# An early activation and a new order for the first stage of a kernel of chunked attention and two feed-forward layers

## The chip, the cores and the metric

The kernel runs on one core of a Trainium2 chip. The metric is the device time of one execution in microseconds (us). Three executions of the kernel before took 1139.6, 1143.71 and 1144.55 us; the median is 1143.71. A core has TensorE (PE: products; its loads of weights are PEld), VectorE (DVE), ScalarE (ACT), GpSimd (POOL) and SyncE (SP, whose queue issues nearly all loads). Each works through its own list of instructions in order and waits for others by semaphores.

## The reference

Three parts follow one another. First, attention in chunks of 32 queries with 16 keys to the left, 8 to the right and 8 memory keys, for 4 batches, 8 heads, 768 positions and 64 channels per head:

```python
for c in range(nc):
    k_full = np.concatenate([mem_k, k_ctx], axis=2)      # 8 + up to 56 keys
    scores = scale * np.matmul(q_c, k_full.transpose(0, 1, 3, 2))
    a = np.exp(scores - np.max(scores, axis=-1, keepdims=True))
    a = a / (np.sum(a, axis=-1, keepdims=True) + 1e-09)
    out[:, :, c_start:c_end] = np.matmul(a, v_full)
```

Its result, seen as x with 3072 rows of 512, goes through two feed-forward layers with 2048 hidden channels:

```python
h = x @ w_in                                  # 3072x512 @ 512x2048
g = s * np.maximum(h, 0.0) ** 2 + b           # first layer
x = g @ w_out                                 # 2048x512
h = x @ moe2_w_in
g = np.maximum(h, 0.0) + alpha * np.minimum(h, 0.0)   # second layer
y = g @ moe2_w_out
```

The weights come as 64-bit floats.

## The kernel before, in words

**Tiles and blocks.** The 3072 rows are 24 tiles of 128 rows, and 6 blocks of four tiles (512 rows). Attention is made tile by tile; the feed-forward layers work on a block at a time. The hidden channels are cut into 16 pieces of 128, called f below. One unit is one block with one piece: a first product (`g1`, line 633, ph), the activation (lines 644 to 677: g, then a high half gh and a low half gl), and a second product (`g2`, lines 692 and 694) that adds to the four banks po. Each product is made of three, high times low, low times high and high times high, so that a unit has 12 matmuls of 512 columns in `g1` and 12 in `g2`. The second product of a unit is placed two units after its first (`LAG`).

**The weights.** A piece has a half for the first product ("w3i" in the lists) and one for the second ("w3o"); pieces 0 and 1 are loaded and converted half by half, the others whole (1.05 MB). `convert` (line 286) turns the 64-bit words into a high and a low 32-bit part in seven steps: magnitude (ScalarE, line 296), clamp, shift, low, sign (VectorE, lines 299, 304, 309, 314), high (ScalarE, line 321) and rest (VectorE, line 327). Two conversions at most can be under way, as their temporary tile has two buffers.

**The attention of a tile.** Loads q (queries and keys, 0.64 MB, lines 376 and 377) and v (0.52 MB, line 384); scores on TensorE (line 401, 128 instructions of TensorE); maxima (line 419), exponentials, sums, reciprocals and normalising (line 475) on VectorE and ScalarE; a turn on TensorE (line 466), copied by ScalarE (line 471); values on TensorE (line 488, 128 instructions); the high half of x by ScalarE (line 520), the low half by VectorE (line 524). A tile in `BY_HEAD` makes its exponentials head by head on ScalarE (line 452, eight activations which also give the sums), another in one activation of 512 columns (line 433) with a subtraction (line 429) and a sum (line 437) on VectorE. There are four sets of buffers for q and v; tile i uses set i mod 4 among the first eight tiles, so v7 needs tile 3's values to be done. Sets 2 and 3 lie in the places of the weights of pieces 13, 14 and 15.

**The first stage.** It makes tiles 0 to 3 (block 0) one by one, then tiles 4 to 7 (block 1) in joint steps of TensorE, each with the scores of one tile and the values of the tile before. The units of block 0 with pieces 0, 1 and 2 (`HALVES`) are cut into a left half of columns, which needs tiles 0 and 1 only, and a right half, which needs tiles 2 and 3. Then come the other pieces below `SEG` for block 0, then all pieces below `SEG` for block 1 (nothing new to convert there), then the pieces from `SEG` on for block 0 and for block 1. Between, the partial sums of both blocks are spilled and later added. From block 2 on all 16 pieces are there, and attention is made two tiles at a time beside the products.

**What sets the order.** All steps are put into a `Plan`, each with its engine, its estimated cost, a rank, and what it waits for. `Plan.order()` (line 147) runs through the plan with these costs and always takes the step that can start first on each engine, ties and readiness by rank (a lower rank goes first). The resulting list is the program's order on each engine. SP's queue is different: it is in order of rank alone, and for the first stage that is the order of `FIRST_LOADS` (line 46). `TILE_RANKS`, `CONV_RANKS` and `STEPS` shift the ranks of the attention tiles, of the conversions and of the steps within a tile. `RATE` is the planner's rate of loads in bytes per us. `Pace` (line 83) is its picture of TensorE: a clock that is slow until a window was busy, and instructions that are fetched in blocks of 256, the first boundary after 184; at each boundary TensorE waits until the block has come, `FETCH` us after it was asked for, by the first figure when no load is under way and by the second when one is. None of these figures is an instruction of the program; they act through the order alone.

Of the kernel before, what the change touches and what calls it, by code (L numbers as in the profile page):

```python
# [9 lines left out]
F32 = mybir.dt.float32  # L10
F32R = mybir.dt.float32r
U32 = mybir.dt.uint32
ACTF = mybir.ActivationFunctionType
# [3 lines left out]
P = 128  # L17
# [14 lines left out]
NEG = -1.0e30  # L32
SCALE = 1.0 / float(D) ** 0.5

SEG = 7
LAG = 2
HALVES = 3
PIECES = 2
# [4 lines left out]
SET_SLOTS = {2: 15, 3: 14}  # L43
QA_SLOT = 13

FIRST_LOADS = """q0 q1 w1i v0 q3 w0o q2 v2 w0i v1 w1o q4 v3 w2 w3 w4 v4 w6 q5 v7 q6 v5 q7 w5 w9 v6 w7 w8""".split()

TILE_RANKS = (-280, -85, -170, -175, -15, -240, -5, -260, -85)

BY_HEAD = (1, 2, 4, 5, 6)  # L50

CONV_RANKS = {1: 195, 2: 35, 3: 30, 4: 25, 5: 20, 6: 15, 9: -40, 10: -95, 11: -25, 12: -10, 13: 40, 14: -70}

STEPS = (28, 18, 18, 47, 43, 38)


KHEAD = LEFT + RIGHT
# [25 lines left out]
class Pace:  # L83


    WINDOW, PHASE = 3.41, 2.7
    BLOCK, FIRST = 256, 184

    def __init__(self):
        self.window, self.active, self.warm = 0, 0.0, False  # L90
# [11 lines left out]
    def run(self, t, step, fetch):  # L102

        done, total = 0, max(step.count, 1)
        while done < total:
            at = self.count + done
            block, into = divmod(at - self.FIRST, self.BLOCK)
            if block >= 0 and into == 0:
                t = max(t, self.due[block])
                self.due[block + 1] = t + fetch(t)  # L110
            n = min(total - done, self.BLOCK - into)
            work = step.cost * n / total
            while work > 1e-9:
                self._to(t + 1e-6)
                speed = 1.0 if self.warm else 0.65 if step.dense else 0.53
                left = self.PHASE + (self.window + 1) * self.WINDOW - t
                took = min(left, work / speed)
                self.active += took * (0.5 if step.dense else 1.0)
                work -= took * speed
                t += took  # L120
            done += n
        self.count += total
        return t


class Plan:
# [1 line left out]

    PAST = {"PE": 0.22, "DVE": 0.15, "ACT": 0.2, "POOL": 0.15, "SP": 2.2, "PQ": 2.2}
    NEXT = {"DVE": 0.12, "ACT": 0.12}  # L130
    RATE = 396e3
    LANES = 8
    FETCH = 2.7, 5.3

    def __init__(self, rings):
        self.steps = []
# [10 lines left out]
    def order(self):  # L147
        for s in self.steps:
            s.n_wait = len(s.after)
            for a in s.after:  # L150
                a.outs.append(s)
        engines = {s.engine for s in self.steps}
        open_ = {e: [] for e in engines}
        for s in self.steps:
            if not s.n_wait:
                open_[s.engine].append(s)
        at = {e: 0.0 for e in engines}
        last = {}
        held = {}
        wire = 0.7  # L160
        landed = [0.0] * self.LANES
        pace = Pace()
        due = sorted((s for s in self.steps if s.engine == "SP"), key=lambda s: (-s.rank, -s.seq))
        done = []
        while len(done) < len(self.steps):
            best = None
            for e in engines:
                pick = None
                queue = [due[-1]] if e == "SP" and due else open_[e]
                for s in queue:  # L170
                    if s.n_wait:
                        continue
                    r = s.ready
                    if s.takes:
                        free = self.free[s.takes[0]]
                        if not free:
                            continue
                        r = max(r, min(free.values()))
                    r = max(r, at[e] + (self.NEXT[e] if e in self.NEXT and last.get(e) in s.after else 0.0))
                    if e == "SP" and s.bytes:  # L180
                        r = max(r, landed[-self.LANES])
                    key = (max(r, at[e] + 0.02), s.rank, s.seq)
                    if pick is None or key < pick[0]:
                        pick = (key, r, s)
                if pick and (best is None or pick[1] < best[1]):
                    best = pick
            assert best, [(e, s.rank, s.takes, s.seq) for e in engines for s in open_[e]]
            _, t, s = best
            e = s.engine
            open_[e].remove(s)  # L190
            if e == "SP":
                due.pop()
            slot = None
            if s.takes:
                ring, holder = s.takes
                free = self.free[ring]
                slot = min(free, key=lambda n: (free[n], n))
                del free[slot]
                held[holder] = (ring, slot)
            s.start = t  # L200
            last[e] = s
            at[e] = pace.run(t, s, lambda t: self.FETCH[wire > t + 1.0]) if e == "PE" else t + s.cost
            end = at[e]
            if s.bytes:
                n = max(1, s.bytes >> 18)
                for k in range(n):
                    wire = max(wire, t + s.cost * (k + 1) / n) + s.bytes / n / self.RATE
                    landed.append(wire + self.PAST[e])
                end = wire
            s.end = end + self.PAST[e]  # L210
            for holder in s.frees:
                ring, n = held.pop(holder)
                self.free[ring][n] = s.end
            for o in s.outs:
                o.n_wait -= 1
                o.ready = max(o.ready, at[e] if o.engine == e in ("PE", "DVE", "ACT") else s.end)
                if not o.n_wait:
                    open_[o.engine].append(o)
            done.append((s, slot))
        return done  # L220
# [3 lines left out]
def tile_chunk_attention_two_ffn(ctx: ExitStack, tc: tile.TileContext, qt, kw, vw, win, wout, cst, out):  # L224
    nc = tc.nc
    const = ctx.enter_context(tc.tile_pool(name="const", bufs=1))
# [13 lines left out]
    plan = Plan({"ph": 2, "g": 2, "gg": 3, "ao": 2})  # L240
# [7 lines left out]
    units = [(0, 0, f, left) for f in range(HALVES)] + [(0, 0, f, right) for f in range(HALVES)]  # L248
    units += [(0, 0, f, full) for f in range(HALVES, SEG)]
    units += [(0, 1, f, full) for f in range(SEG)]  # L250
    units += [(0, j, f, full) for j in range(2) for f in range(SEG, KF)]
    units += [(layer, j, f, full) for layer in range(2) for j in range(2 * (1 - layer), NB) for f in range(KF)]
# [18 lines left out]
    def groups(f):  # L271
        return ((0,), (1,)) if f < SPLIT else ((0, 1),)
# [10 lines left out]
    def first_load(name):  # L283
        return -1000.0 + FIRST_LOADS.index(name)

    def convert(layer, f, mats, rank, after):
# [42 lines left out]
        name = f"w{f}" + ("io"[mats[0]] if n == 1 else "")  # L329
        load = plan.add("SP", 0.45 * n, first_load(name) if layer == 0 and name in FIRST_LOADS else rank - 60 + 14 * mats[0], lambda: load_part(layer, f, mats), after, nbytes=n * (1 << 19))  # L330
        load_done[key] = load
# [198 lines left out]
    def softmax(i, r, sc):  # L530
        a = att[i]
        mx = plan.add("DVE", (0.8 if i % TB in (0, TB - 1) else 0.61) + (0.08 if i in ALONE else 0), r + STEPS[0], lambda: maxima(i), [sc])
        if i in BY_HEAD:
            nm = plan.add("DVE", 0.1, r + STEPS[0], lambda: negate(i), [mx])
            ex = None
            for hp in range(HP):
                ex = plan.add("ACT", 0.58, r + STEPS[1], lambda hp=hp: exps_by_head(i, hp), [nm, ex])
            a["rc"] = plan.add("DVE", 0.32, r + STEPS[2] + 1, lambda: recips(i), [ex])
        else:
# [212 lines left out]

    id_ = plan.add("POOL", 0.6, -1000, lambda: make_identity(nc, ident))
    cs = plan.add("ACT", 0.1, -1000, consts)

    for i in range(TPB):
        attention_alone(i, TILE_RANKS[i])
    for i in range(TPB, 2 * TPB + 1):
        r = TILE_RANKS[i]
        attention(i - 1 if i > TPB else None, i if i < 2 * TPB else None, r, r + 5)  # L760
    slots_free = {f: [x_done[i] for i in range(2 * TPB) if set_of(i) >= OWN_SETS and f in (QA_SLOT, SET_SLOTS[set_of(i)])]
                  for f in (QA_SLOT, *SET_SLOTS.values())}
    for f in range(KF):
        for mats in groups(f):
            convert(0, f, mats, part_when[0, f] - 25 + CONV_RANKS.get(f, 0) + 3 * mats[0], slots_free.get(f, []))

# [8 lines left out]
    for u, (layer, j, f, cols) in enumerate(units):  # L775
        segs.setdefault((layer, j, 0 if layer == 0 and j < 2 and f < SEG else 1), []).append(u)
    seg_of = {u: k for k, us in segs.items() for u in us}
# [39 lines left out]
    for j in range(2, NB):  # L817
        n_units = (KF - SEG) + 7 if j == 2 else KF
        for i in range(j * TPB, j * TPB + TPB, 2):
# [74 lines left out]
    for u in range(n_u):  # L894
        layer, j, f, cols = units[u]
        if layer == 0 and u and units[u - 1][1] == j - 1 and (f == SEG if j == 1 else f == 0 and 2 <= j < NB - 1):
            plan_attention(j + 1)
# [107 lines left out]
```

## Time and profile before

| what | value |
|---|---|
| median of three executions | 1143.71 us (1139.6 to 1144.55) |
| the profiled execution, its time | 1143.53 us |
| its span, first to last instruction | 1141.8 us |
| mean granted clock of TensorE | 0.995 |
| TensorE busy | 1114.9 us (98%) |
| VectorE, ScalarE busy | 605.6 us (53%), 350.8 us (31%) |
| bytes moved by DMA | 98.32 MB |
| TensorE busy from 0 to 5, 10 to 15, 20 to 25 us | 0.29, 1.09, 2.65 us of 5 |
| loads of ScalarE's table | one, 1.28 us, at 8.72 us |

A row of a list of waits reads: engine, result and line, what it waited for, then the total in us, the number of waits and the longest. A row of the timeline reads: start, duration, engine, line, operation, result and operands, and in brackets the idle time before it with what ended it. "issue" is a wait for which the profile shows no releaser. A row of the windows has, for each engine, the busy time and the number of instructions, then TensorE's granted clock, the busy share of the DMA engines and GB/s.

### The profile page before, as it was taken

To read this page: it belongs to the slowest core of one execution; us is meant where nothing else is said; L and a number is where in the kernel's file an instruction comes from. 1 tells how busy PE (TensorE), PEld (TensorE's weight loads), DVE (VectorE), ACT (ScalarE), POOL (GpSimd) and SP (SyncE) were. 2 spreads that over 40 slices of the span, in tenths; PEclk is the share of its full clock that TensorE was granted. 3 is DMA by queue.
4 is the path that set the end of the run, shared out by engine and by line. 5 is a ranking of instruction groups with operands and counts; after the bars stand their busy time and mean duration, and the time that the engine had idled before them with its cause. 6 is when DMAs were issued, how large, how long until landed. Compare 5 with 4: busy or idle time off the path is not lost.

```text
span 1141.8 us, 18302 instructions
## 1 busy us (share of the span) xinstructions
PE 1114.9 (98%) x7848; PEld 925.2 (81%) x7848; DVE 605.6 (53%) x938; ACT 350.8 (31%) x615; POOL 28.8 (3%) x58
## 2 busy tenths in 40 slices
PE   4799999999999999999999999999999999999998
PEld 4788888888888888888888788888888888888886
DVE  6797935445445355434799744334334434344432
ACT  5675644432232223224564311111111111111111
POOL 0000000000000000000000000000000000000000
PEclk9899999999999999999999999999999999999999
DMA  9918121324112213005557103002002002000000
GB/s 348 345 44 303 59 80 66 130 73 148 38 65 92 83 46 112 1 1 189 180 197 251 69 1 111 1 1 102 10 1 92 19 1 91 21 1 2 37 1 37
DMA packets 46241, 98.32 MB, mean 86 GB/s; under 512 B 4944, under 2 KB 4944, under 8 KB 46160
## 3 DMA queue, kind: packets, MB, share of 16 engines
q1 hardware_dynamic: 40320, 77.22, 19.4%
q0 software_dynamic: 5696, 19.93, 4.5%
q8 instruction: 61, 1.00, 0.4%
q14 instruction: 20, 0.16, 0.1%
q10 hardware_dynamic: 144, 0.01, 0.0%
HBM read 76.16 MB, written 20.97 MB: 85 GB/s over the span
## 4 chain that ended last, share of the span: by engine, by line
PE 52%; issue 42%; DMA 3%; DVE 1%; POOL 1%; ACT 1%; SPq 0%; POOLq 0%; ACTq 0%; DVEq 0%
PE ph L633 25%; PE po L694 23%; PE po L692 3%; DMA raw<-in_wout_dram 2%; POOL x1d L731 1%; DMA kv<-in_kw_dram 1%; DMA raw<-in_win_dram 0%; PE sp L488 0%; DVE a L309 0%; DVE a L314 0%; DMA x1d<-o 0%; PE sp L401 0%; DVE gl L677 0%; PE sc L401 0%; PE turns L466 0%
## 5 line engine op out<-in xcount | busy, mean ns | idle before, releaser
L633 PE MATMUL ph<-xh,w 128*128 128x512 f32 (+1 forms) x1560 | 508.4, 388 | 1.1 <-issue 1.1
L633 PEld LDWEIGHTS ph<-xh,w 128*128 128x128 f32 x1560 | 293.4, 189 | 60.9 <-issue 1.4
L633 PE MATMUL ph<-xl,w 128*128 128x512 f32 (+1 forms) x780 | 301.8, 387 | 0.0
L672 ACT ACTIVATE gh<-g 128x512 fp32r<-128x512 f32 (+1 forms) x195 | 121.8, 625 | 462.9 <-DVE g L664 380.4
L692 PE MATMUL po<-gh,w 128*128 128x512 f32 (+1 forms) x792 | 257.5, 387 | 0.1
L694 PE MATMUL po<-w,gh 128*128 128x512 f32 x768 | 251.6, 389 | 1.0 <-DVE o L728 1.0
L677 DVE TENSOR_TENSOR gl<-g,gh 128x512 fp32r<-128x512 f32 (+1 forms) x195 | 133.0, 682 | 106.5 <-ACT gh L672 106.0
L659 DVE TENSOR_SCALAR g<-ph,cst_sb 128x512 f32<-128x512 f32 x96 | 72.0, 750 | 206.6 <-PE ph L633 206.5
L692 PEld LDWEIGHTS po<-gh,w 128*128 128x128 f32 x792 | 148.6, 189 | 30.3 <-DVE o L728 0.7
L633 PEld LDWEIGHTS ph<-xl,w 128*128 128x128 f32 x780 | 147.5, 189 | 29.1
L694 PEld LDWEIGHTS po<-w,gh 128*128 128x128 f32 x768 | 144.1, 188 | 31.6 <-DVE o L728 1.8
L692 PE MATMUL po<-gl,w 128*128 128x512 f32 (+1 forms) x396 | 152.0, 384 | 0.0
L694 PE MATMUL po<-w,gl 128*128 128x512 f32 x384 | 149.4, 389 | 0.0
L644 ACT ACTIVATE g<-ph 128x512 f32<-128x512 f32 (+1 forms) x99 | 57.9, 585 | 156.4 <-PE ph L633 155.1
L651 DVE TENSOR_TENSOR g<-g 128x512 f32<-128x512 f32 x48 | 33.2, 692 | 111.6 <-ACT g L644 111.6
L692 PEld LDWEIGHTS po<-gl,w 128*128 128x128 f32 x396 | 74.9, 189 | 14.2
L694 PEld LDWEIGHTS po<-w,gl 128*128 128x128 f32 x384 | 72.1, 188 | 15.0
L655 DVE TENSOR_SCALAR g<-g,cst_sb 128x512 f32<-128x512 f32 (+1 forms) x99 | 52.9, 534 | 45.1 <-ACT g L649 43.5
L664 DVE SCALAR_TENSOR_TENSOR g<-ph,g 128x512 f32<-128x512 f32 x96 | 66.3, 691 | 3.1
L321 ACT ACTIVATE w<-a 128x1024 fp32r<-128x1024 f32 (+1 forms) x36 | 34.8, 967 | 34.8 <-DVE a L314 33.6
L296 ACT ACTIVATE a<-raw 128x1024 f32<-128x1024 f32 (+1 forms) x36 | 37.6, 1044 | 22.2 <-DVE w L327 13.7
L327 DVE TENSOR_TENSOR w<-a,w 128x1024 fp32r<-128x1024 f32 (+1 forms) x36 | 39.5, 1100 | 3.0 <-ACT w L321 3.0
(81 smaller groups left out, 506.2 us busy)
## 6 DMA issues: line engine op xcount, KB each, us to landing
raw<-in_win_dram SPq DMA_DIRECT2D x64, 256.0 KB, 4.8
raw<-in_wout_dram SPq DMA_DIRECT2D x64, 256.0 KB, 5.2
x1d<-o POOLq DMA_DIRECT2D x24, 512.0 KB, 3.6
vd<-in_vw_dram SPq DMA_DIRECT2D x40, 256.0 KB, 5.6
kd<-in_kw_dram SPq DMA_DIRECT2D x20, 368.0 KB, 4.9
xh<-x1d SPq DMA_DIRECT2D x6, 1024.0 KB, 5.6
xl<-x1d SPq DMA_DIRECT2D x6, 1024.0 KB, 7.7
qT<-in_qt_dram SPq DMA_DIRECT2D x20, 256.0 KB, 4.2
```

The lines of the kernel that those rows point to most:

```text
L296: nc.scalar.activation(out=temp["a"], in_=words(1).bitcast(F32), func=ACTF.Abs)
L321: nc.scalar.activation(out=w[:, :, 0, :], in_=temp["a"], func=ACTF.Copy)
L327: nc.vector.tensor_sub(out=w[:, :, 1, :], in0=temp["a"], in1=w[:, :, 0, :].bitcast(F32))
L633: nc.tensor.matmul(p, lhsT=w[:, a, kk * P:(kk + 1) * P], rhs=x[:, kk, cols], start=(i == 0), stop=(i == 3 * KD - 1))
L644: nc.scalar.activation(out=new_g(u), in_=ph.pop(u), func=ACTF.Relu)
L655: nc.vector.tensor_scalar(out=g, in0=g, scalar1=cst_sb[:, 0:1], scalar2=cst_sb[:, 1:2], op0=ALU.mult, op1=ALU.add)
L659: nc.vector.tensor_scalar(out=new_g(u), in0=ph[u], scalar1=0.0, scalar2=cst_sb[:, 2 + f:3 + f], op0=ALU.min, op1=ALU.mult)
L664: nc.vector.scalar_tensor_tensor(out=g, in0=ph.pop(u), scalar=0.0, in1=g, op0=ALU.max, op1=ALU.add)
L672: nc.scalar.activation(out=gh, in_=gt[u], func=ACTF.Copy)
L677: nc.vector.tensor_sub(out=gl, in0=gt.pop(u), in1=gh.bitcast(F32))
L692: nc.tensor.matmul(po[d][:, cols], lhsT=w[:, a, ds_], rhs=g, start=start, stop=stop)
L694: nc.tensor.matmul(po[d], lhsT=g[:, ds_], rhs=w[:, a, :], start=start, stop=stop)
```

## The change

Three things. First, a tile `zero` of 128x1 is cleared by VectorE at the very beginning, and ScalarE makes an exponential of it right behind the issue of the constants; before, ScalarE's first activation was the first weight's magnitude. Second, the planner's figures: the next block of TensorE's instructions is asked for 48 instructions into the present block and not at its start, `FETCH` goes from 2.7 and 5.3 to 1.6 and 5.1, `RATE` from 396 to 382 kB per us, and one early transfer is held to take 1.2 us longer. Third, the lists that set the order: `SEG` goes from 7 to 9, so that block 0 takes nine pieces before block 1 begins, and `FIRST_LOADS`, `TILE_RANKS`, `BY_HEAD`, `CONV_RANKS` and `STEPS` get new values. The work itself, beside the two small instructions, is the same; the exponentials of tiles 1 and 4 are now made in one activation, those of tiles 3 and 7 head by head.

```diff
-SEG = 7
+SEG = 9
-FIRST_LOADS = """q0 q1 w1i v0 q3 w0o q2 v2 w0i v1 w1o q4 v3 w2 w3 w4 v4 w6 q5 v7 q6 v5 q7 w5 w9 v6 w7 w8""".split()
-TILE_RANKS = (-280, -85, -170, -175, -15, -240, -5, -260, -85)
-BY_HEAD = (1, 2, 4, 5, 6)
-CONV_RANKS = {1: 195, 2: 35, 3: 30, 4: 25, 5: 20, 6: 15, 9: -40, 10: -95, 11: -25, 12: -10, 13: 40, 14: -70}
-STEPS = (28, 18, 18, 47, 43, 38)
+FIRST_LOADS = """q0 q1 w1i q3 v0 w0i q2 v1 w0o w1o v2 q4 w2 w3 w7 w4 v3 w6 v7 w5 q5 v4 w8 w9 q6 q7 v6 v5""".split()
+TILE_RANKS = (-35, -285, -210, -515, -55, -450, -5, -415, -50)
+BY_HEAD = (2, 3, 5, 6, 7)
+CONV_RANKS = {0: -20, 4: 15, 5: -75, 8: 80, 9: -20, 11: 10, 12: 60, 13: -5, 14: -90, 15: -10}
+STEPS = (54, 86, 58, 126, 100, 72)
...
-    BLOCK, FIRST = 256, 184
+    BLOCK, FIRST, AHEAD = 256, 184, 48
...
             if block >= 0 and into == 0:
                 t = max(t, self.due[block])
+            if block >= 0 and into == self.AHEAD:
                 self.due[block + 1] = t + fetch(t)
-            n = min(total - done, self.BLOCK - into)
+            n = min(total - done, self.AHEAD - into if into < self.AHEAD else self.BLOCK - into)
...
-    RATE = 396e3
+    RATE = 382e3
...
-    FETCH = 2.7, 5.3
+    FETCH = 1.6, 5.1
...
-                    wire = max(wire, t + s.cost * (k + 1) / n) + s.bytes / n / self.RATE
+                    wire = max(wire, t + s.cost * (k + 1) / n) + s.bytes / n / self.RATE + (1.2 if len(landed) == self.LANES + 2 else 0.0)
...
+    zero = const.tile([P, 1], F32, name="zero")
+
+    def first_exp():
+
+        nc.scalar.activation(out=zero, in_=zero, func=ACTF.Exp)
+
+    zd = plan.add("DVE", 0.1, -1000, lambda: nc.vector.memset(zero, 0.0))
+    plan.add("ACT", 1.7, -999, first_exp, [zd])
```

## The prediction

> **What bounds the kernel now.** I read the page's busy shares first, then TensorE's waits in two stretches, then the windows of the start.
>
> ```profile
> PE 1114.9 (98%) x7848; PEld 925.2 (81%) x7848; DVE 605.6 (53%) x938; ACT 350.8 (31%) x615; POOL 28.8 (3%) x58
> ```
>
> TensorE lacks 1141.8 - 1114.9 = 26.9 us of the span. Its waits, from 0 to 44 us and from 44 us to the end:
>
> ```profile
> PE sc L401 <- DMA kd<-in_kw_dram: 6.1, 2, 4.7
> PE pt L466 <- DVE e L475: 5.0, 1, 5.0
> PE sp L488 <- issue: 2.5, 1, 2.5
> PE sp L401 <- issue: 2.0, 1, 2.0
> PE sp L401 <- ACT xh L520: 1.8, 1, 1.8
> PE ph L633 <- issue: 1.1, 1, 1.1
> ```
>
> ```profile
> PE po L694 <- DVE o L728: 1.0, 2, 0.5
> PE sp L488 <- ACT qa L471: 0.7, 1, 0.7
> ```
>
> All but 1.7 us of the waits lie in the first 44 us; the rest of the gap is the output at the end. From 43.5 us on TensorE never starves for long, so the change can only shorten, or lengthen, the head. How much the other engines have in hand there is told by the windows (us; busy of PE, PEld, DVE, ACT, POOL; granted clock, DMA share, GB/s):
>
> ```profile
> 35.00:40.00 5.00, 2.86 (x148) 2.50 (x152) 4.96 (x9) 2.43 (x6) 0.00 (x0) 0.88 0.62 204
> 40.00:45.00 5.00, 2.46 (x55) 2.26 (x52) 1.10 (x4) 1.07 (x1) 0.00 (x0) 0.50 1.00 351
> 70.00:75.00 5.00, 5.00 (x142) 4.07 (x141) 5.00 (x8) 3.88 (x6) 0.00 (x0) 1.00 0.01 3
> ```
>
> VectorE is full from 35 to 40 and at 70 us, and nearly empty from 40 to 45. Three facts show that it, and not TensorE's list of work, sets the pace until the second block begins (columns: start, us, what; first the last step of the weights of pieces 5 and 6 with the product that needs each, then the low half of the last tile with the first product of the second block):
>
> ```profile
> 67.90 1.22 DVE L327 TENSOR_TENSOR w<-a,w 128x1024 fp32r<-128x1024 f32 x1
> 69.21 0.47 PE L633 MATMUL ph<-xh,w 128*128 128x512 f32 x1
> 77.11 1.22 DVE L327 TENSOR_TENSOR w<-a,w 128x1024 fp32r<-128x1024 f32 x1
> 78.89 0.39 PE L633 MATMUL ph<-xh,w 128*128 128x512 f32 x1
> 85.90 0.69 DVE L524 TENSOR_TENSOR xl<-sp,xh 128x512 fp32r<-128x512 f32 x1
> 87.57 0.39 PE L633 MATMUL ph<-xh,w 128*128 128x512 f32 x1
> ```
>
> The gaps are 69.21 - 69.12 = 0.1, 0.6 and 1.0 us. So TensorE's head can move forward only as far as VectorE's work does, and VectorE's work moves forward only by its own idle time. Its waits in the first 100 us:
>
> ```profile
> DVE sc L416 <- PE sc L401: 5.9, 1, 5.9
> DVE sp L418 <- PE sp L488: 3.9, 1, 3.9
> DVE a L299 <- ACT a L296: 1.8, 2, 1.5
> DVE g L655 <- ACT g L649: 1.7, 1, 1.7
> DVE gl L677 <- ACT gh L672: 0.7, 1, 0.7
> DVE m L419 <- PE sc L401: 0.7, 1, 0.7
> ```
>
> The first (nothing has landed yet) stays. The other five add up to 8.8 us (a sixth, of 0.3, is left out): **the most that any better order can win** while the same VectorE work stands ahead of the second block.
>
> **The change, part by part.**
>
> *The early activation.* The rows of the first chain:
>
> ```profile
> 7.00 0.75 DVE L429 TENSOR_TENSOR e<-sc,m 128x256 f32<-128x256 f32 x2
> 8.72 1.28 ACT L296 ACT_TABLE_LOAD   x1 [8.72 <-DMA raw<-in_win_dram]
> 10.02 0.66 ACT L296 ACTIVATE a<-raw 128x512 f32<-128x512 f32 x1
> 10.58 0.61 ACT L433 ACTIVATE e<-e 128x512 f32<-128x512 f32 x1
> 13.40 1.09 PE L466 MATMUL pt<-ident,e 128*128 128x128 f32 x4 [4.97 <-DVE e L475]
> ```
>
> Added are a memset of one column and an activation of one column. The trace has neither; the nearest rows, 0.75 us for two operations of 256 columns and 0.61 us for one of 512, bound each at 0 to 0.6 us. Both depend on no load and stand first, so they lie in the 5.9 us before VectorE's first work and the 8.7 us before ScalarE's, and cost nothing; without that cover they would cost up to 1.2 us and the load. The load of 1.28 us leaves the place between VectorE's 7.75 and ScalarE's exponential at 10.58. The exponential can start about 7.9, and the turn of tile 0 comes up to 2.7 us earlier. What counts is VectorE's idle time that this fills: at most 1.5 + 0.7 = 2.2 us (the waits for L296 and for the second scores), at least 0, if the next loads are late. I take the load's own **1.3 us**, as VectorE waited for ScalarE there. The Trainium skill, ScalarE: Activation LUTs, section What ACT_TABLE_LOAD costs, gives 1.28 us and a drain of 1.38 us beside it, 2.66 together; this trace has the first activation at 10.02, which is 8.72 + 1.28 with no drain. By the page this term would be 2.7.
>
> *The order of the loads.* The queue is served in order, so a load takes the place of the one that had as many bytes ahead of it. By the code a q is 0.64 MB, a v or a half weight 0.52, a whole weight 1.05. The old issue times of w0o, w0i, v3 and the first half of w6 (start, us), and the page's row for a v (KB, us to landing):
>
> ```profile
> 5.77 1.70 SPq L280 DMA_DIRECT2D raw<-in_wout_dram  x2
> 10.68 1.65 SPq L280 DMA_DIRECT2D raw<-in_win_dram  x2
> 17.31 0.99 SPq L384 DMA_DIRECT2D kv<-in_vw_dram  x2
> 28.62 1.55 SPq L280 DMA_DIRECT2D raw<-in_win_dram  x2
> ```
>
> ```profile
> vd<-in_vw_dram SPq DMA_DIRECT2D x40, 256.0 KB, 5.6
> ```
>
> w0i moves from 4.65 to 2.97 MB ahead of it, from 10.68 to the old place of w0o at 5.77; v1 from 5.18 to 4.13 MB, which at the 351 GB/s of the window above is 3.0 us. So both things that the first product of block 0 needs are there 3 to 5 us earlier. v3 moves back from 6.87 to 11.06 MB, from 17.31 to the old place of w6 at 28.62; with 5.6 us to land it is there at about 34.2. When it was used before is told by the second of these rows (the first product of block 0, and the values of tile 3):
>
> ```profile
> 26.72 0.58 PE L633 MATMUL ph<-xh,w 128*128 128x256 f32 x1
> 34.91 0.90 PE L488 MATMUL px<-qa,kv 64*64 64x32 f32 x46 [0.25 <-ACT qa L471]
> ```
>
> The values of tile 3 ran at 34.91, so the late v3 costs nothing against before, but it also pins the right half. The new v7 stands one weight behind v3 and uses tile 3's buffer: the whole queue behind it waits until those values are done, about 36. Before, the queue waited at the same place (the window from 35 to 40 has a DMA share of 0.62, so 1.9 us of 5 were lost). Cost of the new loads against before: between 0 and 1.9 us; I take 0. The gain of 3 to 5 us for the left half isn't a term of its own: it lets TensorE fill its early idle time, and is paid out only through VectorE's.
>
> *The corrected instruction fetch.* TensorE's three waits for "issue", 2.5 + 2.0 + 1.1 = 5.6 us, lie, counted in TensorE's instructions (two for each product), at about 696, 952 and 1464, which are 256, and twice 256, apart; I read them as blocks of the program that come late while the loads take all of the DMA engines. The new figures let the planner ask for the next block 48 instructions into the present one. No instruction less is executed, so the boundaries stay; only what stands near them changes. Worst was the wait of 2.5 us that falls into the window from 40 to 45: VectorE's queue stood behind a memset for those scores for 3.9 us, with its other work behind it, and 1.7 us more followed. If the planner now sees it coming it puts conversions there. (TensorE's clock of 0.50 in that window is lost time too, but VectorE sets the pace, so I don't count it again.) Bounds: 0 (an attention product of 128 instructions still takes 1 us, and a block of two still ends before the next has come) and -5.6 us (both VectorE waits gone). Between them I take **-2.5**, since half of these blocks are attention products whichever the order. The Trainium skill, Runtime: NRT & Kernel Launch, section Instruction fetch mechanics, says that the fetch of such blocks is hidden behind the issue of instructions. This trace disagrees, with 2.5 us at one boundary. By the page this term would be 0.
>
> *Nine pieces ahead of the second block, not seven.* TensorE gets two more pieces before tiles 4 to 7 are needed; VectorE gets two more conversions. Steps of a conversion (the mask at line 304 has the shape of the first, the sign at line 314 that of the second), and TensorE's row for a piece from the chain of waits (start, us, what):
>
> ```profile
> 71.23 0.69 DVE L299 TENSOR_SCALAR a<-a 128x1024 f32<-128x1024 f32 x1
> 74.78 1.22 DVE L309 SCALAR_TENSOR_TENSOR a<-raw,a 128x1024 uint32<-128x1024 uint32 x1
> 81.90 1.22 DVE L327 TENSOR_TENSOR w<-a,w 128x1024 fp32r<-128x1024 f32 x1
> ```
>
> ```profile
> 87.73 5.44 PE ph L633 x24
> ```
>
> That is 2 x 0.69 + 3 x 1.22 = 5.0 us. The affine and the low half of the activations add about 1.1 (an estimate: two operations of 512 columns, half of the rows of 1024), and successive operations overlap by near 0.1 each, so some 5.6 us against 5.4 us of TensorE for a piece (24 products, last row, as first and second product have 12 each). A surplus of 0.2 for each of nine pieces gives at most +1.8. But the conversion that ends at 83.1 is the next after that of piece 6 (77.11), and so of a piece that was not needed before the second block: the new order can use that place for one of its two, and against the 5.0 us saved there stand 10.9 us more of TensorE's work as cover, so at best -1.8. Neither end is nearer, and I take **0**.
>
> Sum against the profiled execution (1143.5 us; its span is 1141.8, and 1.7 lie around it): 1143.5 - 1.3 - 2.5 + 0 + 0 = **1139.7 us**. The median of the runs shown, 1143.7, is the same within 0.2. The forecast's own range is 1136 to 1143.
>
> **The rivals.**
>
> *The whole of VectorE's idle time goes.* 1143.5 - 8.8 = 1134.7. For it: w0i and v1 come 3 to 5 us earlier, tile 1's exponential goes off ScalarE's eight small steps, and tiles 4 to 7 move behind the weights. Against it: the right half is pinned by v3 at 34.2, and fetch boundaries remain.
>
> *Only the load of the table is saved.* If the boundaries keep catching the attention products, 1143.5 - 1.3 = 1142.2; with new mismatches of the same size as the gain, 1143.5. The page's rule that the fetch is hidden would end here too.
>
> *The table is loaded twice or more.* One load serves all functions of this trace, with the magnitude first. With the exponential first another set might be chosen, and a change to the other functions would cost 1.28 us each: two early ones give 1143.5 + 1.3 = 1144.8.
>
> *Slower: attention ahead of a conversion that has no slack.* Tiles 3, 5 and 7 get ranks of -515, -450 and -415, far ahead of any weight. If their steps (each tile some 3 us of VectorE, an estimate from five steps of its size such as the low half at 0.69, less overlaps) stand ahead of the conversions of pieces 4 to 8, whose slack was 0.1 and 0.6 us, TensorE runs dry there. The price is one conversion and one tile, 5.0 + 3 = 8, less the 1.3 of the table: 1143.5 + 6.7 = 1150.2. It decides once TensorE has a wait over 3 us for L327 after 45 us. Against it: the loads of q6, q7, v5 and v6 stand last, so these tiles can't begin early.
>
> **How the numbers follow.** Forecast 0.56; all idle time gone 0.15; only the table 0.16; a second load 0.02; slower 0.11. A measurement here tells about 0.5%, 5.7 us, from no change: faster means under 1138.0, slower over 1149.4. Under 1138 falls nearly all of the second case and a third of the forecast's width, 0.14 + 0.19 = 0.33; over 1149.4 the last, which with a like case of another place makes 0.12; within 0.55. The range of 8 in 10 runs from 1134.5, where all of the idle time is won, to 1147.0, within the slower case.
>
> **What would show it.** The table load near 1 us and an exponential at about 8 us: the first step. Turn of tile 0 near 10.7, first product of block 0 near 20 to 22 instead of 26.72: the loads. "Issue" waits of TensorE below 4 us in all and no VectorE wait of 3 us near 40: the fetch. Tile 3's values not before 34; TensorE without a wait over 1 us after 45: the nine pieces. Wrong it would be if TensorE waits for L327 after 45 us, or if VectorE's waits keep a sum of 9 us.

## The result and the profile after

The changed kernel is slower: 1156.61 us (median of four executions, 1154.62 to 1157.17) against 1144.13 for the kernel before, a ratio of 1.0115 with a 95% interval of 1.0086 to 1.0143 (the ratios, here and below, are those on record; they lie within 0.1% of the quotients of the medians). The forecast was 1139.7, with 1147.0 as its upper end.

The busy times in the page of the changed kernel first (the lines of the code stand one further down than before):

```profile
PE 1133.6 (98%) x7848; PEld 926.2 (80%) x7848; DVE 606.2 (52%) x939; ACT 349.4 (30%) x616; POOL 28.7 (2%) x58
```

TensorE has the same 7848 products and is busy 18.7 us longer (1133.6 - 1114.9), while the loads of its weights took the same as before (925.2 and 926.2 in all). So the lost time isn't a wait. The list of TensorE's waits says the same; it's shorter than before:

```profile
PE sc L402 <- DMA kd<-in_kw_dram: 6.3, 2, 4.6
PE pt L467 <- DVE e L476: 5.5, 1, 5.5
PE pt L467 <- ACT a L297: 3.6, 1, 3.6
PE sc L402 <- DVE xl L525: 1.5, 1, 1.5
PE px L489 <- issue: 0.2, 1, 0.2
PE sc L402 <- issue: 0.2, 1, 0.2
```

The waits for issue, 5.6 us in three rows before, are 0.4, and nothing is waited for after 45 us. So the head isn't where the time was lost. Where it went shows in the timeline far behind the first stage, in the second layer. These rows are the first product of each group of 12 in the kernel before (start, us, what; only the rows at which the result changes):

```profile
903.63 0.39 PE L633 MATMUL ph<-xh,w 128*128 128x512 f32 x1
...
906.35 0.39 PE L694 MATMUL po<-w,gh 128*128 128x512 f32 x1
...
909.07 0.39 PE L633 MATMUL ph<-xh,w 128*128 128x512 f32 x1
```

and these are the same in the changed kernel:

```profile
901.35 0.40 PE L634 MATMUL ph<-xh,w 128*128 128x512 f32 x1
...
904.15 0.39 PE L695 MATMUL po<-w,gh 128*128 128x512 f32 x1
...
906.89 0.40 PE L634 MATMUL ph<-xh,w 128*128 128x512 f32 x1
```

Twelve first products took 906.35 - 903.63 = 2.72 us before and 904.15 - 901.35 = 2.80 after; twelve second ones 2.72 before and 2.74 after. All are back to back, at a granted clock of 1.00. Over 192 units that is 192 x (0.08 + 0.02) = 19.2 us. The whole loss is a slower pace of the products of the feed-forward layers, up to the end of the kernel, where the change altered nothing in the work.

What it altered is the memory. In the compiled program the new tile `zero`, 4 bytes per partition rounded up to 32, stands behind the high and low halves of x and ahead of all else: x starts where it did (byte 17120), the weights start at 49920 and not at 49888, and the activations gh at 215552 and not at 215520.

### The profile page after: what moved, and what is told of

The parts are those of the page before. It is cut to its first block, busy times and chain, and to the rows that moved or that the text cites. A ratio compares the mean times of both kernels' runs of the same rounds, so it can differ in the third digit from the quotient of the medians.

```text
span 1155.0 us, 18308 instructions
## 1 busy us (share of the span) xinstructions
PE 1133.6 (98%) x7848; PEld 926.2 (80%) x7848; DVE 606.2 (52%) x939; ACT 349.4 (30%) x616; POOL 28.7 (2%) x58
## 3 DMA queue, kind: packets, MB, share of 16 engines
q1 hardware_dynamic: 40320, 77.22, 19.2%
## 4 chain that ended last, share of the span: by engine, by line
PE 97%; DMA 2%; ACT 1%; DVE 0%; SPq 0%; issue 0%; ACTq 0%
PE ph L634 46%; PE po L693 23%; PE po L695 23%; PE px L489 2%; PE sc L402 1%; DMA raw<-in_wout_dram 1%; PE turns L467 1%; DMA raw<-in_win_dram 1%; DMA kd<-in_kw_dram 0%; PE sp L489 0%; ACT qa L453 0%; PE sp L402 0%; PE pt L467 0%; ACT a L297 0%; SPq L377 0%
## 5 line engine op out<-in xcount | busy, mean ns | idle before, releaser
L634 PE MATMUL ph<-xh,w 128*128 128x512 f32 (+1 forms) x1560 | 517.5, 394 | 0.0
L634 PE MATMUL ph<-xl,w 128*128 128x512 f32 (+1 forms) x780 | 306.6, 393 | 0.1
L328 DVE TENSOR_TENSOR w<-a,w 128x1024 fp32r<-128x1024 f32 (+1 forms) x36 | 39.5, 1100 | 3.0 <-ACT w L322 2.9
```

Of the source, the lines that this page charges most:

```text
L328: nc.vector.tensor_sub(out=w[:, :, 1, :], in0=temp["a"], in1=w[:, :, 0, :].bitcast(F32))
L634: nc.tensor.matmul(p, lhsT=w[:, a, kk * P:(kk + 1) * P], rhs=x[:, kk, cols], start=(i == 0), stop=(i == 3 * KD - 1))
```

## The experiments

Three theories stood against each other. **A**: the products are slower because their operands lie 32 bytes further (A1: because x and the weights no longer stand at the distance that they had, called in step from here on; A2: because of where the weights start). **B**: the new order makes them slower. **C**: the early activation does.

**The new tile elsewhere.** The whole change, with the tile taken from the last pool.

```diff
-    zero = const.tile([P, 1], F32, name="zero")
+    zero = small.tile([P, 1], F32, name="zero")
```

> The changed kernel with one word different: the new tile of one column is taken from the last pool of the on-chip memory and not from the first, so that the weights, the activations and all else that TensorE reads stand at the same addresses as before the change. Theory A (the new tile moved all later tiles by 32 bytes, and TensorE's products in the steady state became slower by that): the 12 first products of a unit go back from 2.80 to 2.72 us and the 12 second ones from 2.75 to 2.72, which takes 15 to 19 us away: 1138 to 1141 us, below before. Theory B (the new order of the first stage, or what it does to the later stage, makes the products slower): as the changed kernel, 1155 to 1157. Theory C (the early activation itself): also 1155 to 1157.

Measured: 1139.26 us, 0.9969 of the kernel before (0.9954 to 0.9985). The pace is back:

```profile
905.46 0.39 PE L634 MATMUL ph<-xh,w 128*128 128x512 f32 x1
...
908.18 0.39 PE L695 MATMUL po<-w,gh 128*128 128x512 f32 x1
...
910.90 0.39 PE L634 MATMUL ph<-xh,w 128*128 128x512 f32 x1
```

2.72 and 2.72 us. B and C fall: with the same order and the same two instructions the loss is gone.

**The kernel before, shifted.** Nothing but an unused tile, with the same order on each engine.

```diff
     xl = [const.tile([P, KD, BLK], F32R, name=f"xl{n}") for n in range(2)]
+    pad = const.tile([P, 1], F32, name="pad")
```

> The kernel before with nothing but an unused tile of one column behind the low halves of x: the order of every engine is that of before, and the weights and activations stand 32 bytes further. Theory A: first products 2.80 us for 12, the second 2.75, and 1143.5 + 192 x 0.08 to 192 x 0.11 = 1159 to 1165 us. Theories B and C: nothing but the addresses changed, so 1143 to 1144.

Measured: 1158.19 us, 1.0129 (1.0093 to 1.0165); 2.80 us for 12 first products, 2.74 for the second. That is just under the 1159 that theory A gave at least. An unused tile that takes 32 bytes costs 1.3%.

**x moved too.** The changed kernel with the tile ahead of x.

```diff
+    zero = const.tile([P, 1], F32, name="zero")
     xh = [const.tile([P, KD, BLK], F32R, name=f"xh{n}") for n in range(2)]
```

> The changed kernel with the new tile ahead of the high halves of x, so that x is moved by the same 32 bytes as the weights and the activations. Theory A1 (slow is a product whose two operands stand 32 bytes apart in a 64-byte line): x and the weights are in step again, first products 2.72 us for 12, 1138 to 1142 us. Theory A2 (slow are weights or activations that start on a multiple of 64 bytes): as the changed kernel, 1155 to 1158. Theories B and C: 1155 to 1157.

Measured: 1138.68 us, 0.9956 (0.9940 to 0.9972), 2.72 and 2.72. The weights stand here exactly where they stand in the slow kernel, so it isn't their own start that makes the products slow: A2 falls, A1 holds.

**x alone moved.** The kernel before with a tile ahead of x and one behind it, so that x moves by 32 bytes and all else by 64.

```diff
+    pad = const.tile([P, 1], F32, name="pad")
     xh = [const.tile([P, KD, BLK], F32R, name=f"xh{n}") for n in range(2)]
     xl = [const.tile([P, KD, BLK], F32R, name=f"xl{n}") for n in range(2)]
+    pad2 = const.tile([P, 1], F32, name="pad2")
```

> The kernel before with an unused tile of one column ahead of x and another behind it: x is moved by 32 bytes, the weights and the activations by 64. Theory A1: x and the weights are out of step, first products 2.80 us for 12, the second, whose operands are both moved by 64, 2.72: 1143.5 + 192 x 0.08 = 1159 us. Theory A2: weights and activations start where they did within a 64-byte line, 1143 to 1145. Theories B and C: 1143 to 1144.

Measured: 1161.98 us, 1.0166 (1.0141 to 1.0191), 2.80 and 2.74. A1 again. The second products, which I expected at 2.72 as their operands stayed in step with each other, are 0.02 slower here too, as in the changed kernel; their first few are slow. That they take this over from the first products ahead of them is only a guess.

**The activations moved.** The kernel before with an unused tile at the head of the working pool: x and the weights in step, gh and gl 32 bytes out of step with the weights.

```diff
+    pad = work.tile([P, 1], F32, tag="pad", name="pad")
```

> The kernel before with an unused tile of one column at the head of the working pool: x and the weights stay in step, the activations gh and gl (and the attention's q, k, v of two sets) are moved by 32 bytes against the weights. Theory A1 for any pair of operands, moving or stationary: now the second products are slow, 2.80 us for 12, the first about 2.72 to 2.75; 1143.7 + 192 x 0.08 to 0.11 = 1159 to 1165 us. If only x against the weights matters: 1143 to 1145.

Measured: 1161.31 us, 1.0162 (1.0137 to 1.0187). Now the second products are the slow ones:

```profile
904.88 0.39 PE L695 MATMUL po<-w,gh 128*128 128x512 f32 x1
...
907.67 0.39 PE L634 MATMUL ph<-xh,w 128*128 128x512 f32 x1
...
910.41 0.39 PE L695 MATMUL po<-w,gh 128*128 128x512 f32 x1
```

2.79 us for the second, 2.74 for the first. It holds in both layers (2.80 in the first), although the weights are the stationary operand of the second product in the first layer and the moving one in the second. So it's the pair that counts, not which of the two is the moving one.

**By how much out of step.** The tile in its place again, but with 16, 32 and 64 columns, which moves weights and activations by 64, 128 and 256 bytes against x.

```diff
-    zero = const.tile([P, 1], F32, name="zero")
+    zero = const.tile([P, 16], F32, name="zero")[:, 0:1]
```

> The changed kernel with 16 columns for the new tile in the place where it stood, so that weights and activations are moved by 64 bytes and not by 32. Theory A1 (64-byte lines, what counts is the difference modulo 64): first products 2.72 us for 12, 1138 to 1141 us. Theory A3 (any difference, or one modulo 128 or more): first products 2.80, 1155 to 1158 us.

> The changed kernel with 32 columns for the new tile in the place where it stood: weights and activations moved by 128 bytes against x. With 32 and 64 bytes the first products took 2.80 us for 12, with 0 they took 2.72. If the period is 128 bytes: 2.72 and 1138 to 1141 us. If it is 256 or more: 2.80 and 1155 to 1158 us.

> The same with 64 columns, 256 bytes. In all kernels so far the weights and the activations stand 1792 bytes apart modulo 2048, which is 7 times 256, and their products were fast: so a period of 256 (or 128) gives 2.72 us for 12 first products and 1138 to 1141 us. If x and the weights must agree modulo more than that, 2.80 and 1155 to 1158 us.

Measured: 64 bytes 1156.55 us, 1.0119 (1.0095 to 1.0142); 128 bytes 1154.22, 1.0105 (1.0073 to 1.0136); 256 bytes 1139.14, 0.9969 (0.9953 to 0.9986). My 64-byte line was wrong; the period that fits is 256 bytes (128 bytes came out 0.8 us under the range that I gave for it). The rows for 128 bytes:

```profile
899.65 0.40 PE L634 MATMUL ph<-xh,w 128*128 128x512 f32 x1
...
902.44 0.39 PE L695 MATMUL po<-w,gh 128*128 128x512 f32 x1
```

and for 256:

```profile
900.34 0.39 PE L695 MATMUL po<-w,gh 128*128 128x512 f32 x1
...
903.06 0.39 PE L634 MATMUL ph<-xh,w 128*128 128x512 f32 x1
...
905.78 0.39 PE L695 MATMUL po<-w,gh 128*128 128x512 f32 x1
```

2.79 us for the first products with 128, 2.72 with 256. All runs on this question together (the times of a group are read from the starts of rows in both layers, and agree to 0.02, where two figures stand they are those of the first and of the second layer):

| kernel | weights against x, bytes | gh against weights | 12 first, us | 12 second, us | ratio |
|---|---|---|---|---|---|
| before | 0 | 0 | 2.72 | 2.72 | 1 |
| changed | 32 | 0 | 2.80 | 2.74 | 1.0115 |
| tile elsewhere | 0 | 0 | 2.72 | 2.72 | 0.9969 |
| before, shifted | 32 | 0 | 2.80 | 2.74 | 1.0129 |
| x moved too | 0 | 0 | 2.72 | 2.72 | 0.9956 |
| x alone moved | 32 | 0 | 2.80 | 2.74 | 1.0166 |
| activations moved | 0 | 32 | 2.76, 2.74 | 2.80, 2.79 | 1.0162 |
| 64 bytes | 64 | 0 | 2.80 | 2.74 | 1.0119 |
| 128 bytes | 128 | 0 | 2.79 | 2.74 | 1.0105 |
| 256 bytes | 256 | 0 | 2.72 | 2.72 | 0.9969 |

The columns give the difference beyond that of the kernel before, in which x and the weights stand a multiple of 2048 bytes apart, and gh and the weights 7 times 256 beyond one.

**The early activation alone**, on the kernel before, with no address moved.

```diff
+    zero = small.tile([P, 1], F32, name="zero")
+    def first_exp():
+        nc.scalar.activation(out=zero, in_=zero, func=ACTF.Exp)
+    zd = plan.add("DVE", 0.1, -1000, lambda: nc.vector.memset(zero, 0.0))
+    plan.add("ACT", 1.7, -999, first_exp, [zd])
```

> The kernel before with the early activation alone, its one-column tile taken from the last pool so that no operand of TensorE moves; figures, lists and order as before. By the prediction's first term 1143.7 - 1.3 = 1142.4 us, between 1141.5 (all of VectorE's two early waits) and 1143.7 (the later steps, whose order is unchanged, wait for loads anyway). The load of the table stands near 1 us.

Measured: 1143.13 us, 0.9999 (0.9981 to 1.0016): nothing that can be told from no change. ScalarE's start in this run, and two of TensorE's waits:

```profile
1.18 1.28 ACT L759 ACT_TABLE_LOAD   x1 [1.18 <-PEq L997]
2.47 0.20 ACT L759 ACTIVATE zero<-zero 128x1 f32<-128x1 f32 x1
9.03 0.66 ACT L296 ACTIVATE a<-raw 128x512 f32<-128x512 f32 x1 [6.35 <-DMA raw<-in_win_dram]
9.59 0.61 ACT L433 ACTIVATE e<-e 128x512 f32<-128x512 f32 x1
```

```profile
PE sp L488 <- issue: 4.0, 1, 4.0
PE pt L466 <- DVE e L475: 3.5, 1, 3.5
```

The load went to 1.18 us and cost nothing there. But the old order has the first weight's magnitude ahead of the exponential, and that waits for its load to 9.03: the exponential came 1.0 us earlier (9.59 for 10.58), the turn's wait fell from 5.0 to 3.5, and the later wait for issue grew from 2.5 to 4.0. VectorE's wait of 3.9 us for the same products grew to 5.2. The gain was given back.

**The order alone**, without the tile and the activation.

```diff
-    zd = plan.add("DVE", 0.1, -1000, lambda: nc.vector.memset(zero, 0.0))
-    plan.add("ACT", 1.7, -999, first_exp, [zd])
```

> The changed kernel without the early activation and its tile: the new figures, lists and order alone, all addresses as before. By the prediction's other terms 1143.7 - 2.5 = 1141.2 us; if the early activation is worth nothing, as the run with the tile elsewhere, 1139.3. The load of the table stands behind the first thing that ScalarE waits for.

Measured: 1139.93 us, 0.9973 (0.9959 to 0.9987). That is the whole gain of the version with the tile elsewhere; the early activation adds nothing that these intervals can tell.

**Seven pieces again**, all else as in the changed kernel, the tile elsewhere.

```diff
-SEG = 9
+SEG = 7
```

> The changed kernel with its tile elsewhere (addresses as before) and SEG back at 7, all other lists and figures as in the changed kernel. The prediction gave the nine pieces 0 (between +1.8 and -1.8): 1139.3, between 1137.5 and 1141. If the nine pieces carry the gain of the new order, 1143 or more.

Measured: 1148.87 us, 1.0051 (1.0031 to 1.0071). Against 0.9969 the nine pieces are worth 0.8%, some 9 us, together with these lists. One wait of TensorE is new, for a tile's turn, put down to a conversion's step on ScalarE:

```profile
PE turns L467 <- ACT w L322: 4.0, 1, 4.0
```

The windows of this run tell where the 9 us went. TensorE is busy for 1.00 us of the 5 from 85 to 90 us, and for 3.59 of the 5 from 90 to 95; its granted clock is 0.50 from 90 to 95 and 0.64 from 95 to 100. With nine pieces it is busy for 5.00 of 5 at a clock of 1.00 in all three windows. The idle time is 4.0 + 1.4 us, and the low clock behind it costs some 3.6 more (an estimate: 3.59 x 0.50 + 5.00 x 0.36), 9.0 together.

**The old figures**, all else as in the changed kernel, the tile elsewhere.

```diff
-    RATE = 382e3
+    RATE = 396e3
-    FETCH = 1.6, 5.1
+    FETCH = 2.7, 5.3
-            if block >= 0 and into == self.AHEAD:
-                self.due[block + 1] = t + fetch(t)
+                self.due[block + 1] = t + fetch(t)
```

> The changed kernel with its tile elsewhere and the planner's old figures for fetch, rate and the late transfer, all lists as in the changed kernel. If the figures carry the gain, as the prediction's second term had it (2.5 us, by placing work at the fetch boundaries): 1141.8 or more, and waits of TensorE for issue of 5 us in all. If the lists carry it: 1139 to 1140.

Measured: 1143.59 us, 1.0019 (1.0003 to 1.0034), 0.5% behind the same lists with the new figures. So the lists alone don't carry the gain. Nor is it shown that the fetch carries it: this run's waits for issue are 1.1 us, not the 5 I expected. Other waits stand in their place:

```profile
PE pt L466 <- ACT w L321: 5.6, 1, 5.6
PE pt L466 <- DVE rs L457: 2.9, 1, 2.9
PE sp L401 <- DMA kd<-in_kw_dram: 2.0, 2, 1.8
```

Lists and figures belong together: ranks found under one set of figures make another order under the other.

## Why the prediction was wrong

**The step that failed** is the early activation's "cost nothing". I costed its two instructions and the place that covers them, and put its tile at nothing without a word on it. That tile takes 32 bytes ahead of the weights, and 12 first products then take 2.80 us and not 2.72. This one line is worth the difference between 0.9969 and 1.0115, some 17 us, and it alone turned a small gain into a loss. The sum by the pace, 19.2 us, is 2 us more; the interval of 1.0115, some 3 us either way, leaves that open, and whether a slower product costs less in the head no run shows. None of my rivals had it: I took from the waits that the change could act only on the head, and that holds for an order, not for an allocation. The rival on the slower side (attention ahead of a conversion, 1150) didn't occur: TensorE waits for no L328 after 45 us.

**The rest of the sum came out, in part by luck.** With the addresses kept, the change takes 1139.26 us, where the sum said 1139.7. But two of its terms were sized wrongly, in opposite ways, and the reasons given for them held only in part:

- The table, -1.3: measured alone 0.9999, -0.1 us (between -2 and +2), and nothing on top of the new order. The mechanism was right in its first step: in the changed kernel the exponential of tile 0 starts at 7.68 us, where I had 7.9. But the turn of tile 0, which I put at 10.7, starts later than before. The rows of the changed kernel:

```profile
7.68 0.63 ACT L434 ACTIVATE e<-e 128x512 f32<-128x512 f32 x1 [5.01 <-DVE e L430]
...
14.14 1.94 PE L467 MATMUL pt<-ident,e 128*128 128x128 f32 x8 [5.52 <-DVE e L476]
```

What stands between is seen best in the version with the tile elsewhere, where VectorE has the same order here (the sum of tile 0's exponentials, then the normalising of tiles 0 and 1, then the turn of both):

```profile
8.46 0.69 DVE L438 TENSOR_REDUCE rs<-e 128x8 f32<-128x512 f32 x1 [0.75 <-ACT e L434]
...
13.46 1.24 DVE L476 TENSOR_TENSOR e<-e,rs 128x512 f32<-128x512 f32 x2
14.25 1.94 PE L467 MATMUL pt<-ident,e 128*128 128x128 f32 x8 [5.40 <-DVE e L476]
```

The turn starts before the second of the two normalising steps has ended (13.46 + 1.24 = 14.70), so it waited for tile 0's own. Between the sum and that step the new order gives VectorE the maxima, the subtraction and the sum of tile 1 and four steps of a conversion: 5.0 us lie between their starts, where it was 1.3 before (11.23 to 12.57). The exponential came 2.9 us earlier, and VectorE's order used that up. The first product of block 0 came at 25.27 us and not at 20 to 22: of the 3 to 5 us that I took from v1 and w0i, 1.5 were left.

- The order, -2.5 for the fetch and 0 for the nine pieces: measured -3.1 us alone (0.9973; between -1.5 and -4.7). That I booked all of it to the fetch is borne out only in part. In the version with the tile elsewhere the waits for issue are 0.8 us in two rows, and VectorE's wait of 3.9 us is gone. But VectorE's other waits hardly shrank (the first 100 us):

```profile
DVE sc L417 <- PE sc L402: 5.0, 1, 5.0
DVE g L656 <- ACT g L650: 2.3, 1, 2.3
DVE a L300 <- ACT a L297: 2.0, 2, 1.4
DVE xl L525 <- ACT xh L521: 1.8, 2, 1.5
DVE zero L762 <- PEq L998: 0.8, 1, 0.8
DVE rs L438 <- ACT e L434: 0.8, 1, 0.8
DVE w L328 <- ACT w L322: 0.7, 2, 0.4
DVE gl L678 <- ACT gh L673: 0.5, 1, 0.5
```

The first and the one for `zero` are the start, 5.8 us where it was 5.9. The other six are 8.1 us, against 8.8 and 0.3 before. By my rule, that TensorE's head moves forward only as VectorE's idle time shrinks, the gain would have been 1.0 us at most. In the changed kernel these waits even add up to 12.1 us, so one of my two signs of being wrong was there; 5.0 of them end at 99.95 us, while TensorE waits for nothing after 45. What did shrink is TensorE's own idle time: 18.7 us from 0 to 60 where it was 21.0, and none from 80 to 85 where it was 0.7.

The rule also had its condition beside it, "while the same VectorE work stands ahead of the second block", and the nine pieces break it: they give TensorE 10.9 us more to do before tiles 4 to 7 must be ready. VectorE's windows from 90 to 100 us, first before and then in this version, show it nearly full and then with time in hand:

```profile
90.00:95.00 5.00, 5.00 (x24) 4.14 (x23) 4.67 (x6) 4.58 (x7) 0.00 (x0) 1.00 0.86 307
95.00:100.00 5.00, 5.00 (x23) 4.14 (x23) 4.96 (x7) 3.23 (x6) 0.68 (x1) 1.00 1.05 396
```

```profile
90.00:95.00 5.00, 5.00 (x84) 4.03 (x83) 3.54 (x5) 3.21 (x6) 0.00 (x0) 1.00 0.00 0
95.00:100.00 5.00, 5.00 (x24) 4.10 (x23) 0.69 (x1) 1.23 (x3) 0.68 (x1) 1.00 0.78 239
```

That seven pieces with the same lists cost 0.8%, as TensorE runs dry at 85 us, goes the same way. How much of it is the pieces and how much the lists made for nine stays open.

**What held.** The late v3: the values of tile 3 ran with tile 2's from 34.41 us on (I had 34.2 for its landing, and no cost). The queue stood still behind v7 until those values were done:

```profile
30.66 1.02 SPq L281 DMA_DIRECT2D raw<-in_wout_dram  x2
37.69 1.32 SPq L385 DMA_DIRECT2D kv<-in_vw_dram  x2
```

and it cost nothing that shows: of TensorE's waits none after 8 us is put down to a load. One table load serves all functions with the exponential first too: 1.28 us at 1.18, the first activation at 2.47, again with no drain between. Here the Trainium skill, ScalarE: Activation LUTs, section What ACT_TABLE_LOAD costs, gives a drain of 1.38 us more. No such time shows behind the load in this trace; ScalarE was idle ahead of it, and what a load costs behind other work no run here shows.

## What to carry to other kernels

A new tile, however small, moves all that is allocated behind it. Where TensorE is the bound, look after such an edit at the start times of a group of products far from the edit, before looking for waits: here the same products, back to back at a clock of 1.00, ran at another pace, and it was the place of their operands that had changed. With operands like these, put small helper tiles in a pool behind the operands of the products, or keep the operands of a product a multiple of 256 bytes apart. Of the versions run, the change with its tile elsewhere, with x moved too or with a tile of 256 bytes is a little faster than the kernel before (0.9969, 0.9956 and 0.9969, whose intervals overlap and lie below 1).

## What the hardware showed that I had not expected

With 32-bit operands, 512 moving columns and 128 stationary ones, a product whose two operands start a multiple of 256 bytes apart (as in the kernel before, and with 256 bytes more) follows the one before after 2.72 / 12 = 0.227 us. With 32, 64 or 128 bytes more between them it takes 2.80 / 12 = 0.233 us, 3% more, at the same granted clock of 1.00. Moving both by 32 bytes changed nothing (x moved too), and it made no difference which of the two was moved. It holds in both layers, for first products (x against the weights) and for second ones (gh and gl against the weights, 32 bytes only). Why the chip does this no run shows; other shapes, types and differences were not tried, so a period of 256 bytes is what fits these five and no more, nor was it tried whether the attention's small products gain or lose by it. After a group out of step the next group, itself in step, is slower by 0.01 to 0.04 us for 12; what carries it over is open.
